# Half of O by wide matmuls, and sum p·dp by VectorE, in a one-query attention backward

One Trainium2 chip, one core of it. The metric is the device time of one execution, in microseconds (us); lower is better.

## The reference, cut to what matters

```python
B, H, Sq, Skv, Dh = 1, 32, 1, 8192, 128            # q, k, v, grad_out: bfloat16

def _fwd_reference(q, k, v):
    scores = jnp.einsum('bhqd,bhkd->bhqk', q, k) * q.shape[-1] ** -0.5
    attn = _softmax(scores, axis=-1)
    return jnp.einsum('bhqk,bhkd->bhqd', attn, v)

_out, _vjp = jax.vjp(_fwd_reference, q, k, v)
return (_out, *_vjp(grad_out))                     # O, dq, dK, dV
```

For every head one query meets 8192 keys. With p the softmax, O = p·V, dp = V·dO, ds = p·(dp − sum p·dp), dq = ds·K, and the outer products dK = ds⊗q and dV = p⊗dO. K and V are read (134 MB), dK and dV are written (134 MB). The sum of p·dp over the keys equals O·dO. The kernel before takes it as O·dO, the changed kernel as sum p·dp.

## The kernel before

A head is four 2 MB transfers: K and V in, dK and dV out. Each is cut into sixteen shares (the trace has sixteen completion records a transfer). I take each to be one DMA engine's: a share of 128 KB takes 4.87 us in the steady stretch, 27 GB/s, and sixteen of these are the 427 GB/s of the page. What waits for a transfer waits for its slowest share: in the changed kernel a store that waited for an earlier one was issued at 374.06 us, when that one's slowest share had landed at 374.0 and the next at 368.5. The parts that the argument touches:

```python
K_BUFS = 3
V_BUFS = 2
# ... (cut)
    for h in range(H + 1):
        p_ = h - 1
        if h < H:
            rows_bc(h)                     # q and dO broadcast to all partitions, copy qd on ScalarE
            for u in range(NCH):
                k_blocks(h, u)             # K transposes on VectorE, four of 1.2 us
            k_scores(h)                    # scores on TensorE
        # ... (cut)
        if h > 0:
            ds_of(p_)                      # needs O.dO of the head before, in m[:, 1]
            outer(p_, "dk", 0)             # dK in four parts on VectorE, then a 2 MB store
            dq_of(p_, 0)
        # ... (cut: softmax of head h, its maxima and sums across partitions)
        v_transposes(h, 0); v_transposes(h, 1); v_transposes(h, 2)       # fp32 transposes on TensorE
        contract(Vt[h], x["p"], x["m"][:, 2:3])      # O: 64 matmuls with one moving column each
        nc.scalar.copy(o_all[:, h:h + 1], x["m"][:, 2:3])
        v_scores(h, 0); v_scores(h, 1)               # dp
        v_transposes(h, 3)
        nc.tensor.matmul(x["m"][:, 1:2], lhsT=do_f[:, h:h + 1].to_broadcast([P, P]),
                         rhs=o_all[:, h:h + 1], start=True, stop=True)   # O.dO on every partition
        v_scores(h, 2); v_scores(h, 3)
        outer(h, "dv", 0); outer(h, "dv", 1); outer(h, "dv", 2)          # dV, then a 2 MB store
        load_v(h + 2)
        outer(h, "dv", 3)
```

Of the kernel before, what the change touches and what calls it, by code (L numbers as in the profile page):

```python
# [9 lines left out]
ALU = mybir.AluOpType  # L10
AX = mybir.AxisListType
BF16 = mybir.dt.bfloat16
F32 = mybir.dt.float32
PSUM = bass.MemoryType.PSUM

CH = 16
R = 4
K_BUFS = 3
V_BUFS = 2
QD = 32  # L20


@with_exitstack
def kernel(
# [11 lines left out]
    nc = tc.nc  # L36
    P = 128
    _, H, S, D = k.shape
    assert D == P and S % (P * CH) == 0 and H <= P
    NT = S // P  # L40
    NCH = NT // CH
# [4 lines left out]
    scale = float(D) ** -0.5  # L46

    consts = ctx.enter_context(tc.tile_pool(name="consts", bufs=1))
# [3 lines left out]
    tpool = ctx.enter_context(tc.tile_pool(name="tsb", bufs=3))  # L52
    gpool = ctx.enter_context(tc.tile_pool(name="gen", bufs=2))
    small = ctx.enter_context(tc.tile_pool(name="small", bufs=2))
    psT = ctx.enter_context(tc.tile_pool(name="psT", bufs=2, space=PSUM))
    psS = ctx.enter_context(tc.tile_pool(name="psS", bufs=1, space=PSUM))
    psD = ctx.enter_context(tc.tile_pool(name="psD", bufs=2, space=PSUM))
# [30 lines left out]
    ident = consts.tile([P, P], BF16)  # L88
# [31 lines left out]


    twice = consts.tile([H, 2, 2, W], BF16)
    do_f = consts.tile([P, H], F32)

    def do_columns():
        for e2 in range(2):
            nc.scalar.copy(
                twice[:, e2], rows[:, 1, :].rearrange("h (j e) -> h e j", e=2)[:, e2:e2 + 1, :].to_broadcast([H, 2, W]))
        tp = psT.tile([P, CH, P], BF16, tag="T", name="tp_do")
        for e2 in range(2):  # L130
            nc.tensor.transpose(tp[:, e2, 0:H], twice[:, e2].rearrange("h t j -> h (t j)"), ident[0:H, 0:H])
        nc.tensor.transpose(tp[:, 2, 0:H], rows[:, 1, :], ident[0:H, 0:H])
        for e2 in range(2):
            for t in range(2):
                nc.scalar.copy(do_blk[t * W:(t + 1) * W, :, e2, t], tp[t * W:(t + 1) * W, e2, 0:H])
        nc.scalar.copy(do_f[:], tp[:, 2, 0:H])

    o_all = consts.tile([P, H], F32)
    dq_all = consts.tile([P, H], F32)

    def k_blocks(h, u):


        if u == 0:
            XK[h] = ktpool.tile([P, CH, NB, NCH, QD], F32, tag="XK", name="XK_sb")
        nc.vector.transpose(XK[h][:, :, :, u, :],  # L146
                            slots(Kt[h], u, NCH).rearrange("p g d -> p (g d)").bitcast(F32).rearrange(
                                "p (g w j) -> p g w j", g=CH, w=NB))

    def k_scores(h):  # L150
        x = st[h]
        out = x["s"][:, 0:NT].rearrange("p (a g) -> p g a", a=NQ)
        cols = XK.pop(h).rearrange("p g w u i -> p (g w u i)").bitcast(BF16).rearrange(
            "p (g w ui e) -> p g w e ui", g=CH, w=NB, e=2)
        for g in range(CH):
            for c in range(2 * NB):
                nc.tensor.matmul(out[:, g, :], lhsT=cols[:, g, c // 2, c % 2], rhs=q_blk[:, h, c, :],  # L157
                                 start=(c == 0), stop=(c == 2 * NB - 1), skip_group_check=True)
# [18 lines left out]
    def v_transposes(h, c):  # L177

        T_ps = psT.tile([P, CH // 2, P], F32, tag="T", name="T_ps")
        words = Vt[h].rearrange("p n d -> p (n d)").bitcast(F32)  # L180
        for i in range(CH // 2):
            m = c * CH // 2 + i
            nc.tensor.transpose(T_ps[:, i, :], words[:, m * P:(m + 1) * P], ident_f[:])  # L183
        X = tpool.tile([P, CH // 2, P], F32, tag="XT", name="XT_sb")
        nc.scalar.copy(X[:], T_ps[:])  # L185
        XV[h, c] = X
# [11 lines left out]
    def contract(Xt, rep, out_col, first=0, last=NT):  # L198
        for n in range(first, last):
            nc.tensor.matmul(out_col, lhsT=Xt[:, n, :], rhs=rep[:, n, 0:1],  # L200
                             start=(n == 0), stop=(n == NT - 1), skip_group_check=True)

    def outer(h, which, r):
        x = st[h]
        if r == 0:
            x[which] = gpool.tile([P, NT, D], BF16, tag=which, name="G_" + which)
        G, dst = x[which], out_2 if which == "dk" else out_3
        rep, row = x["ds"] if which == "dk" else x["p"], x["qd"][:, 0 if which == "dk" else 1, :]
        Q = NT // 4
        nc.vector.tensor_tensor(  # L210
            slots(G, r, 4).rearrange("p n (a b) -> p n a b", b=R),
            slots(rep, r, 4).unsqueeze(2).to_broadcast([P, Q, D // R, R]),
            row.rearrange("p (a b) -> p a b", b=R).unsqueeze(1).to_broadcast([P, Q, D // R, R]),
            op=ALU.mult)
        parts = 1
        if h == 0 or h == H - 1:
            parts = 2
        if r % (4 // parts) == 4 // parts - 1:
            c = r // (4 // parts)
            nc.sync.dma_start(rows_of(dst, h, c, parts), slots(G, c, parts))  # L220
# [19 lines left out]
    def dq_of(h, half):  # L240
        out = st[h]["dp"][:, 128:129]
        contract(Kt[h], st[h]["ds"], out, half * NT // 2, (half + 1) * NT // 2)
        if half == 1:
            nc.scalar.copy(dq_all[:, h:h + 1], out)  # L244
# [10 lines left out]
    for h in range(H + 1):  # L255
        p_ = h - 1
        if h < H:
            x = st[h] = {}
            rows_bc(h)
            for u in range(NCH):  # L260
                k_blocks(h, u)
            k_scores(h)
        if h == 0:
            do_columns()
        if h > 0:
            ds_of(p_)
            outer(p_, "dk", 0)
            dq_of(p_, 0)
        if h < H:
            s_mask(h)  # L270
            s_swap(h)
        if h > 0:
            dq_of(p_, 1)
            outer(p_, "dk", 1)
        if 0 < h and h + 2 < H:
            load_k(h + 2)
        if h < H:
            mx = small.tile([P, 1], F32, tag="mx")
            nc.vector.reduce_max(mx[:], x["sn"], axis=AX.X)
            top = small.tile([P, 1], F32, tag="top")  # L280
            nc.vector.tensor_scalar_mul(top[:], mx[:], scale)
            x["m"] = psM.tile([P, 512], F32, tag="m", name="m_ps")
            nc.tensor.transpose(x["m"][:, 128:256], top[:].to_broadcast([P, P]), ident_f[:])
        if h > 0:
            outer(p_, "dk", 2)
        if h == 0:
            load_k(2)
        if h < H:
            nbias = small.tile([P, 1], F32, tag="nbias")
            nc.vector.tensor_reduce(nbias[:], x["m"][:, 128:256], axis=AX.X, op=ALU.max, negate=True)  # L290
            e = small.tile([P, NT], F32, tag="e")
            rs = small.tile([P, 1], F32, tag="rs")
            nc.scalar.activation(e[:], x["sn"], ACT.Exp, bias=nbias[:], scale=scale, accum_out=rs[:])  # L293
            nc.tensor.matmul(x["m"][:, 0:1], lhsT=ones_f[:], rhs=rs[:], start=True, stop=True,  # L294
                             skip_group_check=True)
        if h > 0:
            outer(p_, "dk", 3)
        if h == H:
            break
        rinv = small.tile([P, 1], F32, tag="rinv")  # L300
        nc.vector.reciprocal(rinv[:], x["m"][:, 0:1])  # L301
        x["p"] = small.tile([P, NT, R], BF16, tag="prep", name="p_rep")
        nc.scalar.activation(x["p"][:], e[:].unsqueeze(2).to_broadcast([P, NT, R]), ACT.Copy, scale=rinv[:])  # L303
        x["p_s"] = small.tile([P, NT], F32, tag="p_s", name="p_s")
        nc.vector.tensor_scalar(x["p_s"][:], e[:], rinv[:], scale, op0=ALU.mult, op1=ALU.mult)
        v_transposes(h, 0)
        v_transposes(h, 1)
        v_transposes(h, 2)
        contract(Vt[h], x["p"], x["m"][:, 2:3])
        nc.scalar.copy(o_all[:, h:h + 1], x["m"][:, 2:3])  # L310
        v_scores(h, 0)
        v_scores(h, 1)
        v_transposes(h, 3)
        nc.tensor.matmul(x["m"][:, 1:2], lhsT=do_f[:, h:h + 1].to_broadcast([P, P]), rhs=o_all[:, h:h + 1],
                         start=True, stop=True, skip_group_check=True)
        v_scores(h, 2)
        v_scores(h, 3)
        outer(h, "dv", 0)
        outer(h, "dv", 1)
        outer(h, "dv", 2)  # L320
        if 0 < h and h + 2 < H:
            load_v(h + 2)
        outer(h, "dv", 3)
        if h == 0:
            load_v(2)
        if h == H - 1:
            result(o_all, out_0)

    result(dq_all, out_1)
    order.__exit__(None, None, None)  # L330


# [28 lines left out]
```

## Time and profile before

| | before |
|---|---|
| time, median of the first three runs (range) | 646.29 us (646.24 to 646.5) |
| span of the profiled run, mean granted TensorE clock | 644.5 us, 0.600 |
| busy: TensorE, VectorE, ScalarE | 75%, 78%, 28% |
| data queue | 268.47 MB, 98.2% of sixteen engines |
| instruction queue (q8) | 75 packets, 1.23 MB |

A share of 98.2% over sixteen engines says that the transfers bound the kernel. It doesn't say which engine ends last, and that is what the time is. For that one reads the windows of the tail, where a share of 0.06 means one engine of sixteen.

One view that the prediction doesn't show becomes important. It is the chain of waits of the kernel before around 100 us (columns: start, duration, what ran):

```profile
101.31 0.58 PE m_ps L294 x2
101.90 4.09 PE T_ps L183 x24
105.98 1.59 PE m_ps L200 x64
...
117.49 0.35 PE dp_ps L200 x8
117.87 28.45 DMA Kt<-in_k_dram
146.34 4.62 DVE XK_sb L146 x4
```

Up to 117.9 us the chain goes through TensorE, ScalarE and VectorE: the first transfers run ahead, and compute sets the pace of the heads (17.2 us, from one exponential to the next). From there on, the chain goes through a wait for K in every second head, and a head takes 19.8 us. I call the two stretches "compute paces" and "transfers pace".

### The profile page before, as it was taken

The page shows a single profiled execution, that of the slowest core. Times are in us where ns is not written, and L with a number is a line of the kernel's source. Part 1 is how long each engine was busy: PE and PEld are TensorE (multiplying, and loading weights), DVE is VectorE, ACT ScalarE, POOL GpSimd, SP SyncE. Part 2 cuts the span into 40 slices and gives each one's busy share as a digit, 9 for nine tenths or more (in the row PEclk, how much of TensorE's full clock was granted, in tenths as well). Part 3 has the DMA queues.
Part 4 walks back from the last instruction along what each step waited for, and adds up shares of the span by engine and source line. Part 5 has one row for each costly group of instructions (what it writes and reads, how often), then busy time and mean ns, then how long its engine had stood idle before and what let it go on. Part 6 is the DMA issues. An engine that isn't in the chain of part 4 may idle for free.

```text
span 644.5 us, 20935 instructions
## 1 busy us (share of the span) xinstructions
PE 481.0 (75%) x9673; PEld 452.0 (70%) x9673; DVE 505.5 (78%) x653; ACT 183.5 (28%) x332; POOL 0.7 (0%) x6
## 2 busy tenths in 40 slices
PE   3898888886677877768777787667786777877780
PEld 2888888886677866768666777667785676866670
DVE  5989899867977779777788777797767977778860
ACT  2333333332233222233222332223322223222230
POOL 0000000000000000000000000000000000000000
PEclk9766666655666655666556666556655666655665
DMA  8999999999999999999999999999999999999985
GB/s 349 407 425 430 424 425 423 429 426 431 427 428 427 427 427 429 429 429 425 433 422 433 425 430 427 427 429 425 427 429 425 431 425 429 429 427 430 424 365 238
DMA packets 19718, 269.80 MB, mean 419 GB/s; under 512 B 2352, under 2 KB 2352, under 8 KB 2864
## 3 DMA queue, kind: packets, MB, share of 16 engines
q1 hardware_dynamic: 19584, 268.47, 98.2%
q8 instruction: 75, 1.23, 0.7%
q14 instruction: 11, 0.09, 0.0%
q10 hardware_dynamic: 48, 0.01, 0.0%
HBM read 134.23 MB, written 134.23 MB: 417 GB/s over the span
## 4 chain that ended last, share of the span: by engine, by line
DMA 59%; PE 21%; DVE 14%; ACT 2%; issue 1%; SPq 0%; DVEq 0%; ACTq 0%
DMA Kt<-in_k_dram 48%; DVE XK_sb L146 8%; PE T_ps L183 8%; DMA out_dram<-G_dv 5%; DMA out_dram<-G_dk 5%; PE s_ps L157 5%; DVE G_dk L210 4%; PE dp_ps L200 3%; PE m_ps L200 2%; PE dp_ps L195 2%; ACT XT_sb L185 1%; PE m_ps L294 1%; DVE G_dv L210 1%; PE s_ps L173 1%; DVE sm L163 1%
## 5 line engine op out<-in xcount | busy, mean ns | idle before, releaser
L210 DVE TENSOR_TENSOR G_dv<-p_rep,qd 128x2048 bf16<-128x2048 bf16 x128 | 148.2, 1221 | 90.3 <-DMA out_dram<-G_dv 84.6
L183 PE MATMUL T_ps<-ident_f,Vt 128*128 128x128 f32 x1024 | 203.4, 382 | 0.2 <-PE m_ps L294 0.2
L183 PEld LDWEIGHTS T_ps<-ident_f,Vt 128*128 128x128 f32 x1024 | 190.7, 210 | 0.2 <-issue 0.2
L185 ACT COPY XT_sb<-T_ps 128x1024 f32<-128x1024 f32 x128 | 128.6, 1013 | 129.3 <-PE T_ps L183 127.2
L210 DVE TENSOR_TENSOR G_dk<-ds_rep,qd 128x2048 bf16<-128x2048 bf16 x128 | 155.6, 1218 | 2.9 <-DMA out_dram<-G_dk 1.9
L146 DVE STREAM_TRANSPOSE XK_sb<-Kt 128x1024 f32<-128x1024 f32 x128 | 148.3, 1214 | 5.8 <-DMA Kt<-in_k_dram 4.7
L157 PEld LDWEIGHTS <-XK_sb 128*128 128x128 bf16 x2048 | 57.7, 104 | 90.7 <-DVE pdt L234 79.9
L157 PE MATMUL s_ps<-q_blk,XK_sb 128*128 128x4 bf16 x2048 | 59.7, 168 | 82.1 <-DVE pdt L234 72.1
L195 PE MATMUL dp_ps<-do_blk,XT_sb 128*128 128x2 bf16 x2048 | 66.7, 164 | 18.1 <-ACT XT_sb L185 18.1
L195 PEld LDWEIGHTS <-XT_sb 128*128 128x128 bf16 x2048 | 64.9, 102 | 20.7 <-ACT XT_sb L185 20.7
L200 PE MATMUL dp_ps<-ds_rep,Kt 128*128 128x1 bf16 x2048 | 64.1, 165 | 1.3 <-issue 1.0
L200 PEld LDWEIGHTS <-Kt 128*128 128x128 bf16 x2048 | 59.6, 104 | 6.8 <-issue 6.6
L244 ACT COPY dq_all<-dp_ps 128x1 f32<-128x1 f32 x32 | 5.1, 159 | 192.4 <-PE dp_ps L200 178.5
L200 PEld LDWEIGHTS <-Vt 128*128 128x128 bf16 x2048 | 57.7, 97 | 0.9
L200 PE MATMUL m_ps<-p_rep,Vt 128*128 128x1 bf16 x2048 | 56.9, 164 | 0.0
L294 PEld LDWEIGHTS m_ps<-rs,ones_f 128*128 128x128 f32 x64 | 16.0, 311 | 49.9 <-ACT e L293 49.9
L294 PE MATMUL m_ps<-rs,ones_f 128*128 128x1 f32 x64 | 18.8, 362 | 40.5 <-ACT e L293 40.5
L303 ACT ACTIVATE p_rep<-e,rinv 128x256 bf16<-128x256 f32 x32 | 16.3, 508 | 30.1 <-DVE rinv L301 30.1
L163 DVE TENSOR_TENSOR sm<-s_ps,in_quad 128x256 f32<-128x256 f32 x32 | 13.6, 424 | 11.1 <-PE s_ps L157 7.9
L229 ACT CAST qd<-s_ps 128x256 bf16<-128x256 f32 x32 | 11.9, 372 | 32.2 <-PE s_ps L225 32.2
L236 DVE SCALAR_TENSOR_TENSOR ds_rep<-dp_ps,pdt,p_s 128x256 bf16<-128x256 f32 x32 | 15.5, 484 | 5.2 <-PE dp_ps L195 2.4
L293 ACT ACTIVATE e<-s_ps,nbias 128x64 f32<-128x64 f32 x32 | 10.0, 313 | 31.8 <-DVE nbias L290 31.8
(44 smaller groups left out, 143.4 us busy)
## 6 DMA issues: line engine op xcount, KB each, us to landing
Vt<-in_v_dram SPq DMA_DIRECT2D x32, 2048.0 KB, 30.0
Kt<-in_k_dram SPq DMA_DIRECT2D x31, 2048.0 KB, 30.8
out_dram<-G_dv SPq DMA_DIRECT2D x30, 2048.0 KB, 34.6
out_dram<-G_dk SPq DMA_DIRECT2D x30, 2048.0 KB, 33.6
out_dram<-G_dv SPq DMA_DIRECT2D x4, 1024.0 KB, 15.0
out_dram<-G_dk SPq DMA_DIRECT2D x4, 1024.0 KB, 13.3
Kt<-in_k_dram SPq DMA_DIRECT2D x4, 512.0 KB, 5.1
out_dram<-fin_sb SPq DMA_DIRECT2D x2, 8.0 KB, 13.1
```

Source lines behind the costliest of these rows:

```text
L146: nc.vector.transpose(XK[h][:, :, :, u, :], slots(Kt[h], u, NCH).rearrange("p g d -> p (g d)").bitcast(F32).rearrange("p (g w j) -> p g w ...
L157: nc.tensor.matmul(out[:, g, :], lhsT=cols[:, g, c // 2, c % 2], rhs=q_blk[:, h, c, :], start=(c == 0), stop=(c == 2 * NB - 1), skip_group ...
L163: nc.vector.tensor_tensor(x["sm"][:], x["s"][:, 0:NT].rearrange("p (a g) -> p a g", a=NQ).unsqueeze(2) .to_broadcast([P, NQ, NCH, CH]), in ...
L183: nc.tensor.transpose(T_ps[:, i, :], words[:, m * P:(m + 1) * P], ident_f[:])
L185: nc.scalar.copy(X[:], T_ps[:])
L195: nc.tensor.matmul(st[h]["dp"][:, n:n + 2], lhsT=X[:, i, e2, :], rhs=do_blk[:, h, e2, :], start=(e2 == 0), stop=(e2 == 1), skip_group_chec ...
L200: nc.tensor.matmul(out_col, lhsT=Xt[:, n, :], rhs=rep[:, n, 0:1], start=(n == 0), stop=(n == NT - 1), skip_group_check=True)
L210: nc.vector.tensor_tensor(slots(G, r, 4).rearrange("p n (a b) -> p n a b", b=R), slots(rep, r, 4).unsqueeze(2).to_broadcast([P, Q, D // R, ...
L229: nc.scalar.copy(x["qd"][:].rearrange("p a d -> p (a d)"), x["s"][:, 256:512])
L236: nc.vector.scalar_tensor_tensor(out=x["ds"][:], in0=x["dp"][:, 0:NT].unsqueeze(2).to_broadcast([P, NT, R]), scalar=pdt[:], in1=x["p_s"][: ...
L294: nc.tensor.matmul(x["m"][:, 0:1], lhsT=ones_f[:], rhs=rs[:], start=True, stop=True, skip_group_check=True)
L303: nc.scalar.activation(x["p"][:], e[:].unsqueeze(2).to_broadcast([P, NT, R]), ACT.Copy, scale=rinv[:])
```

## The change

Its intent: fewer TensorE instructions (32 narrow O matmuls become 8 wide ones), and no dependence of ds on O. A wide matmul takes four keys' columns of p as weights and four tiles of V as 512 moving columns. Only the four diagonal 128-column blocks of the 4x512 result are O. They lie on four partitions, so they are sent through a DRAM scratch and summed once at the end. The last head keeps narrow matmuls and does them behind its dq.

```diff
+    def o_wide(h, first, last):
+        x = st[h]
+        for g in range(first, last):
+            nc.tensor.matmul(x["s"][0:R, :], lhsT=x["p"][:, R * g:R * (g + 1), 0],
+                             rhs=Vt[h][:, R * g:R * (g + 1), :].rearrange("p n d -> p (n d)"),
+                             start=(g == 0), stop=(g == WIDE // R - 1), skip_group_check=True)
+        if last == WIDE // R:
+            four = fours.tile([R, R * D], F32, tag="four", name="four")
+            nc.scalar.copy(four[:], x["s"][0:R, :])
+            nc.sync.dma_start(scratch[h, 0:R * R * D].rearrange("(a c) -> a c", a=R), four[:])
+    def pd_of(h):
+        # ... (cut: tiles)
+        nc.vector.tensor_tensor_reduce(out=junk[:], in0=x["p_s"][:], in1=x["dp"][:, 0:NT], scale=1.0,
+                                       scalar=0.0, op0=ALU.mult, op1=ALU.add, accum_out=pd[:])
+        nc.tensor.matmul(x["m"][:, 1:2], lhsT=ones_s[:], rhs=pd[:], start=True, stop=True, ...)
 # ... (cut; in the loop over the heads)
-            for u in range(NCH):
+            for u in range(NCH - 1):
                 k_blocks(h, u)
+        if h > 0:
+            pd_of(p_)
+        if h < H:
+            k_blocks(h, NCH - 1)
 # ...
         v_transposes(h, 1)
+        if h < H - 1:
+            o_wide(h, 0, 8)
         v_transposes(h, 2)
-        contract(Vt[h], x["p"], x["m"][:, 2:3])
-        nc.scalar.copy(o_all[:, h:h + 1], x["m"][:, 2:3])
+        if h < H - 1:
+            o_narrow(h, WIDE)
 # ...
-        nc.tensor.matmul(x["m"][:, 1:2], lhsT=do_f[:, h:h + 1].to_broadcast([P, P]), rhs=o_all[:, h:h + 1], ...)
 # ... (cut: behind V of the last head, the read-back; at the end, sum, transpose and store of O)
+            nc.sync.dma_start(blocks[0:h], scratch[0:h].rearrange("h (a c) -> h a c", a=R)[:, :, 0:D])
+    nc.vector.reduce_sum(block_sum[:], blocks[:].rearrange("h a d -> h d a"), axis=AX.X)
```

More of the change, by code (lines that the diff above doesn't have):

```diff
@@ L20 @@
 QD = 32
+WIDE = 32
 @with_exitstack
@@ L54 @@
     small = ctx.enter_context(tc.tile_pool(name="small", bufs=2))
+    fours = ctx.enter_context(tc.tile_pool(name="fours", bufs=3))
+    dram = ctx.enter_context(tc.tile_pool(name="scr", bufs=1, space=bass.MemoryType.DRAM))
     psT = ctx.enter_context(tc.tile_pool(name="psT", bufs=2, space=PSUM))
@@ L122 @@
     twice = consts.tile([H, 2, 2, W], BF16)
-    do_f = consts.tile([P, H], F32)
     def do_columns():
@@ L131, in do_columns @@
             nc.tensor.transpose(tp[:, e2, 0:H], twice[:, e2].rearrange("h t j -> h (t j)"), ident[0:H, 0:H])
-        nc.tensor.transpose(tp[:, 2, 0:H], rows[:, 1, :], ident[0:H, 0:H])
         for e2 in range(2):
@@ L135, in do_columns @@
                 nc.scalar.copy(do_blk[t * W:(t + 1) * W, :, e2, t], tp[t * W:(t + 1) * W, e2, 0:H])
-        nc.scalar.copy(do_f[:], tp[:, 2, 0:H])
+    ones_s = consts.tile([P, P], F32)
+    nc.vector.memset(ones_s[:], 1.0 / scale)
+    blocks = consts.tile([H, R, D], F32)
+    nc.vector.memset(blocks[:], 0.0)
+    scratch = dram.tile([H, R * (R + 1) * D], F32, name="scratch")
     o_all = consts.tile([P, H], F32)
@@ L201, in contract, with o_narrow @@
                              start=(n == 0), stop=(n == NT - 1), skip_group_check=True)
+    def o_wide(h, first, last):
[8 more added lines that the diff above has]
+            nc.sync.dma_start(scratch[h, 0:R * R * D].rearrange("(a c) -> a c", a=R), four[:])
+    def o_narrow(h, first):
+        x = st[h]
+        for n in range(first, NT):
+            nc.tensor.matmul(x["m"][:, 2:3], lhsT=Vt[h][:, n, :], rhs=x["p"][:, n, 0:1],
+                             start=(n == first), stop=(n == NT - 1), skip_group_check=True)
+        nc.scalar.copy(o_all[:, h:h + 1], x["m"][:, 2:3])
+    def pd_of(h):
+        x = st[h]
+        junk = small.tile([P, NT], F32, tag="junk")
+        pd = small.tile([P, 1], F32, tag="pd")
+        nc.vector.tensor_tensor_reduce(out=junk[:], in0=x["p_s"][:], in1=x["dp"][:, 0:NT], scale=1.0,
+                                       scalar=0.0, op0=ALU.mult, op1=ALU.add, accum_out=pd[:])
+        nc.tensor.matmul(x["m"][:, 1:2], lhsT=ones_s[:], rhs=pd[:], start=True, stop=True, skip_group_check=True)
     def outer(h, which, r):
@@ L273 @@
             dq_of(p_, 1)
+            if h == H:
+                o_narrow(p_, 0)
             outer(p_, "dk", 1)
@@ L313 @@
         v_transposes(h, 3)
-        nc.tensor.matmul(x["m"][:, 1:2], lhsT=do_f[:, h:h + 1].to_broadcast([P, P]), rhs=o_all[:, h:h + 1],
-                         start=True, stop=True, skip_group_check=True)
         v_scores(h, 2)
@@ L326 @@
         if h == H - 1:
-            result(o_all, out_0)
+            nc.sync.dma_start(blocks[0:h], scratch[0:h].rearrange("h (a c) -> h a c", a=R)[:, :, 0:D])
     result(dq_all, out_1)
+    block_sum = consts.tile([H, D], F32)
+    nc.vector.reduce_sum(block_sum[:], blocks[:].rearrange("h a d -> h d a"), axis=AX.X)
+    fin_ps = psT.tile([P, CH // 2, P], F32, tag="T", name="fin_o")
+    nc.tensor.transpose(fin_ps[0:H, 0, :], o_all[:], ident_f[:])
+    o_sb = consts.tile([H, D], BF16)
+    nc.vector.tensor_tensor(o_sb[:], fin_ps[0:H, 0, :], block_sum[:], op=ALU.add)
+    nc.sync.dma_start(out_0.rearrange("b h s d -> (b h s) d"), o_sb[:])
     order.__exit__(None, None, None)
```

## The prediction

The sum came to **647.4 us**, the mean of two cases. To the 646.3 us of before it added -0.9 for instruction packets, +2.9 for the scratch stores (31 times 84 + 9 ns, on four engines) and +3.2 for the read-back (124 times 26 ns, on one engine). The first case assumed without a trace that the read-back lies on one of the four engines of the stores and that this engine is one of the eight that carry instruction packets: 646.3 - 0.9 + 2.9 + 3.2, less 2.1, the average lead of a late engine on the latest, is 649.4. The second, "if not", gave 645.4. A sign that the first had come: a very low DMA share for several us at the end.

Three figures that the text takes for granted were measured in the traces of the two kernels. Wide matmuls of 512 columns start 427 ns apart at a granted clock of 0.5 and 216 ns at 1.0 (medians of 38 and 138 in the changed kernel), so eight are 3.4 and 1.7 us. There are 258 TensorE rows to an instruction packet before (19,384 to 75) and 256 after (17,894 to 70), and with five packets fewer went 1271 instructions fewer of all engines, 254 a packet. And the denser work was granted the full clock more often: 31 stretches of 6.8 us and one of 3.4, for 32 of 3.4 before, or 0.68 on average for 0.60.

> **What bounds the kernel now.** I read the page first (engine shares, slices, queues), then the windows of the tail, then the chain in order of time, then the packets of the trace. Lines of the page:
>
> ```profile
> PE 481.0 (75%) x9673; PEld 452.0 (70%) x9673; DVE 505.5 (78%) x653; ACT 183.5 (28%) x332; POOL 0.7 (0%) x6
> DMA  8999999999999999999999999999999999999985
> GB/s 349 407 425 430 424 425 423 429 426 431 427 428 427 427 427 429 429 429 425 433 422 433 425 430 427 427 429 425 427 429 425 431 425 429 429 427 430 424 365 238
> q1 hardware_dynamic: 19584, 268.47, 98.2%
> q8 instruction: 75, 1.23, 0.7%
> DMA 59%; PE 21%; DVE 14%; ACT 2%; issue 1%; SPq 0%; DVEq 0%; ACTq 0%
> L200 PE MATMUL m_ps<-p_rep,Vt 128*128 128x1 bf16 x2048 | 56.9, 164 | 0.0
> ```
>
> No compute engine is above 78%, and the DMA engines are busy from the second slice to the last but one, at about 427 GB/s. 268.47 MB at that rate are 629 us of a 644.5 us span, so only some 15 us are not plain transfer. The two last slices show where: 365 and 238 GB/s. The windows there (columns: PE, PEld, DVE, ACT, POOL busy, clock, DMA share, GB/s):
>
> ```profile
> 632.00:634.00 2.00, 0.00 (x0) 0.00 (x0) 0.00 (x0) 0.00 (x0) 0.00 (x0) 0.50 0.93 387
> 634.00:640.00 6.00, 0.00 (x0) 0.00 (x0) 0.00 (x0) 0.00 (x0) 0.00 (x0) 0.50 0.56 235
> 640.00:642.00 2.00, 0.00 (x0) 0.00 (x0) 0.00 (x0) 0.00 (x0) 0.00 (x0) 0.50 0.19 79
> ```
>
> From 634 to 640 us the share is 0.56 with nothing left to compute: about nine of sixteen engines still work and seven are done. The completion records of each transfer in the trace (sixteen, one an engine) say the same. At the first whole V they lie within 0.6 us of each other, at a transfer near 130 us within 4.7, near 330 within 9, and of the last dK store seven come at 633.7 and nine between 639.9 and 643. The lag grows in jumps of about 1.5 us, one about every 9 us, in turn on eight engines. That is the pace of the q8 packets (75 in 644 us, 16 KB each, 1.0 us a packet against 0.61 for a data packet; the data packet after one is also stretched to 1.0 to 1.1). So the end is set by **the slowest DMA engine**: its share of the data and its 8 to 10 instruction packets. Had it idle time? The tail of the chain says no:
>
> ```profile
> 608.95 0.02 DVEq L210
> 609.02 0.36 DVE G_dk L210
> 614.45 5.22 PE T_ps L183 x24
> 619.67 1.62 PE m_ps L200 x64
> 625.33 1.22 DVE G_dk L210
> 627.69 2.27 DVE G_dk L210 x2
> ```
>
> The last compute goes from a store's landing at 608.9 to the issue of dK of the last head at 627.7 (18.8 us). The slowest engine then still has six shares of 2 MB before that store, at 4.87 us each 29 us, to 638. Last-head compute has 10 us of slack.
>
> [...] The trace's clock is 0.60 on average (one 3.4 us window in five or six at full); 24 fp32 transposes took 5.13 us at half clock, 214 ns each[...].
>
> **The change part by part** (31 of 32 heads; the last keeps narrow matmuls).
> - *Removed on TensorE*: 32 of 64 narrow O matmuls a head. 56.9 / 2048 = 27.8 ns each, 0.89 us a head. Also the matmul of o with dO in its old place (L314, 0.23 to 0.43 us on the chain).
> - *Added on TensorE*: 8 matmuls of 512 columns: 3.4 us at half, 1.7 at full clock; I take 2.6 since they sit in the densest stretch. Net +1.7 us a head, PE busy about 530 us. Beside the transfers.
> - *VectorE*: a product-and-sum over 128x64, estimated 0.3 us from the 128x64 row of L305 (0.26) plus an accumulator read; 10 us in all, DVE about 515 us. It stands before the fourth K transpose and waits for dp. In a compute-bound head the fourth transpose (1.16) thus slips behind dp: about +0.85 us. In the steady state K arrives last, and it is +0.3.
> - *ScalarE*: a copy of 4x512 from PSUM, about 0.59 us between the rows of 256 (0.37) and 1024 columns (1.01). 18 us in all; idle anyway.
> - *Head period*: early heads, before the transfers pace them, ran every 17.2 us; steady ones every 19.8 (K loads of the chain at 155.1, 194.9, 234.5: 39.7 for two). With +1.7, +0.85, -0.3: 19.5. Just hidden, and the 10 us slack covers an excess of 0.3 us a head.
> - *Instruction packets*: TensorE's list shrinks from 16,660 to 15,200 rows; the other engines add about 190. (1460 - 190) / 256 = 5.0 packets fewer, 0.6 on each of eight engines, x 1.5 = **-0.9 us**. This is the change's whole gain on the bound.
> - *Scratch stores*: per head one 2 KB packet on four engines. 8 KB took 309 ns, 4 KB 159, so 2 KB about 84 plus 9 for the semaphore[...].
> - *Read-back*: [...] A 256 B packet took 18 ns, so about 26[...].
> - *Result O at the end*: sum, transpose and store follow the read-back, but its packet queues behind dK like the old result's: about 0. *O of the last head behind dq*: takes 1.6 us from a chain with slack: 0.
>
> [...] If not, the fast engines' 6 us of reserve (and what they starve anyway) swallow both: **645.4**. At half each: **647.4**.
>
> **The rivals.**
> (a) *Compute becomes the bound.* For it: a period of 19.5 beside 19.8 is close, and a head at half clock throughout would cost 0.8 more. Against it: denser work should be granted full clock more often, and the tail has 10 us of slack. At 20.3 us a head the compute would end 15 to 20 us later, minus the slack: 652 to 656. I give an effect over 2% 3 in 100.
> (b) *A wait in the DMA queue.* In the new order each transfer also waits for the eighth before it; with five a head instead of four, dV's store waits for dK's store of two heads before, which landed 5 us later than the old issue. For it: real waits will appear on SP. Against it: five 2 MB transfers (24 us) stay queued on the slowest engine, so it never starves. Worth 0 to 2 us.
> (c) *The designer's gain*: fewer instruction packets and an early last dK give 2 us or more (643 to 644). For it: the 1.5 us jumps are real. Against it: only five packets go, and the tail's chain has slack.
>
> **Range and chances.** The two cases give 645.4 and 649.4; the packet count per engine is worth a packet (1.5 us) either way; the small transfers may cost twice my estimate (+3), and (a) has a tail upward. Range 644.0 to 652.5. Beyond 2% would be 633 or 659: the first needs less data, the second (a) in full.
>
> **What would show each step.** Right: q8 falls from 75 to about 70 packets; GB/s stays near 427; the last windows still show half of the engines working alone; PE busy near 530. [...] Wrong: DMA share below 0.95 in mid-run, the chain full of PE and DVE rows instead of K loads, a head period of 20 or more, or q8 unchanged.

## The result, and the profile after

The changed kernel is correct and took **652.37 us** (median of 4, 651.64 to 652.71) beside 646.26 us for the kernel before in the same rounds. The ratio is 1.0095, 95% interval [1.0077, 1.0112]. A ratio is the mean time of one kernel's runs over that of the other's of the same rounds, so it is not quite the ratio of the medians. A change below 2% was foretold and came. The range held the time, but near its upper end: +6.1 us where +1.1 was predicted. That it held was luck: its upper part was kept for small transfers at twice their cost and for compute as the bound, and neither came.

The page of the changed kernel, the lines that answer to those shown of before:

```profile
PE 513.3 (79%) x8928; PEld 424.1 (65%) x8928; DVE 513.3 (79%) x721; ACT 198.8 (31%) x360; POOL 0.7 (0%) x6
GB/s 335 421 429 421 424 419 422 425 426 430 424 428 425 418 422 427 429 427 425 428 427 427 424 431 427 424 427 429 427 426 426 430 429 423 425 429 428 398 367 157
q1 hardware_dynamic: 19957, 268.79, 97.6%
q8 instruction: 70, 1.15, 0.7%
DMA 45%; PE 32%; DVE 13%; issue 4%; ACT 3%; SPq 0%; DVEq 0%; ACTq 0%
L212 PE MATMUL s_ps<-Vt,p_rep 128*4 128x512 bf16 x248 | 72.7, 446 | 0.0
L217 ACT COPY four<-s_ps 4x512 f32<-4x512 f32 x31 | 17.8, 576 | 39.1 <-PE s_ps L212 39.1
```

In mid-run the GB/s are what they were. They fall in the last slices: 398, 367, 157. On the chain, DMA has dropped from 59% to 45% and PE has risen from 21% to 32%. The windows of the tail (columns as in the prediction):

```profile
638.00:640.00 2.00, 0.00 (x0) 0.00 (x0) 0.23 (x1) 0.00 (x0) 0.00 (x0) 0.50 0.79 327
640.00:642.00 2.00, 0.00 (x0) 0.00 (x0) 0.00 (x0) 0.00 (x0) 0.00 (x0) 0.50 0.42 172
642.00:644.00 2.00, 0.00 (x0) 0.00 (x0) 0.00 (x0) 0.00 (x0) 0.00 (x0) 0.50 0.06 25
644.00:646.00 2.00, 0.00 (x0) 0.00 (x0) 0.00 (x0) 0.00 (x0) 0.00 (x0) 0.50 0.07 29
646.00:648.00 2.00, 0.00 (x0) 0.00 (x0) 0.00 (x0) 0.00 (x0) 0.00 (x0) 0.50 0.06 25
```

Before, nine engines shared the last stretch. Now **one engine works alone for over 6 us**, at 25 to 29 GB/s. The completion records agree. Of the last dK store's sixteen shares, before, the slowest came at 643.2 us, the next at 642.9 and the fastest at 633.9. After, the slowest came at 649.1, the next at 642.4 and the fastest at 639.2. Fifteen engines have ended by 642.4, a little sooner than before; the last one ends 5.9 us later than the last one did, and that is the change in time. I call this engine Y. The trace doesn't number the engines. But the landings of one transfer can be matched with those of the next (an inference, by the smallest changes): in the changed kernel three engines stay fast, four fall back from them by 4.0 to 8.5 us up to head 31, eight show seven to nine jumps of over 0.9 us, as an instruction packet leaves one (such a packet takes 1.0 us for the 611 ns of a data packet of the same 16 KB, and behind 66 of the 70, behind 74 of the 75 before, a data packet of over 0.9 us starts within 60 ns), and Y is the sixteenth. So I take the four to be those of the scratch stores, and Y not to be one of them; from 136 us on Y shows one such jump (at 395 us).

The landings show when Y falls behind. The times are completion records of the slowest share and the next, whichever engine's, of the same loads of V, in us:

| V of head | before: slowest | before: next | after: slowest | after: next |
|---|---|---|---|---|
| 4 | 75.3 | 74.6 | 74.8 | 74.7 |
| 7 | 136.0 | 135.1 | 136.3 | 135.1 |
| 10 | 196.1 | 194.9 | 197.6 | 195.1 |
| 13 | 255.5 | 254.7 | 259.3 | 255.0 |
| 19 | 374.3 | 374.2 | 378.9 | 374.9 |
| 25 | 493.9 | 493.8 | 499.1 | 493.3 |

From head 7 to head 13 the slowest share took (255.5 − 136.0) / 6 = 19.9 us a head before and (259.3 − 136.3) / 6 = 20.5 after. The next share kept its pace: 19.9 and 20.0. (Before head 7 several engines land within 0.3 us, and the slowest need not be Y.) From head 13 to head 25 the slowest took 19.9 and 20.0. So Y loses some 0.6 us a head up to about 260 us, which makes 3.8 of the 5.9 us by head 13; the rest comes more slowly behind it (4.6 by head 19, 5.2 by head 25).

The chain of waits after (columns: start, duration, what ran) shows what else ends there:

```profile
223.38 3.52 PE T_ps L188 x16
226.89 2.77 PE s_ps L212 x8
229.66 1.02 PE T_ps L188 x8
...
257.91 0.94 PE dp_ps L205 x32
258.88 30.43 DMA Kt<-in_k_dram
...
298.23 30.77 DMA Kt<-in_k_dram
```

Compute paces the heads until 258.9 us instead of 117.9. The wide matmuls (1.8 to 2.8 us for eight) stand on this chain. The period in that stretch is 18.3 and 19.3 us in turn, 18.8 on average, for 14 heads; before it was 17.2 us for seven.

### The profile page after: what moved, and what is told of

Its sections match the earlier page's. It is cut to its first block, busy times and chain, and to the rows that moved or that the text cites. A ratio compares the mean times of both kernels' runs of the same rounds, so it can differ in the third digit from the quotient of the medians. Undisturbed runs are those within 1.5% of the kernel's fastest.

```text
span 650.9 us, 19664 instructions
## 1 busy us (share of the span) xinstructions
PE 513.3 (79%) x8928; PEld 424.1 (65%) x8928; DVE 513.3 (79%) x721; ACT 198.8 (31%) x360; POOL 0.7 (0%) x6
## 4 chain that ended last, share of the span: by engine, by line
DMA 45%; PE 32%; DVE 13%; issue 4%; ACT 3%; SPq 0%; DVEq 0%; ACTq 0%
DMA Kt<-in_k_dram 44%; PE T_ps L188 12%; PE s_ps L162 7%; DVE XK_sb L151 6%; PE s_ps L212 5%; DVE G_dk L242 4%; PE dp_ps L200 3%; PE dp_ps L205 3%; ACT XT_sb L190 2%; PE m_ps L223 2%; PE m_ps L332 1%; DMA blocks<-scratch 1%; ACT e L331 1%; DVE sm L168 1%; PE s_ps L178 1%
## 5 line engine op out<-in xcount | busy, mean ns | idle before, releaser
L188 PE MATMUL T_ps<-ident_f,Vt 128*128 128x128 f32 x1024 | 185.0, 350 | 0.2 <-PE m_ps L332 0.2
L188 PEld LDWEIGHTS T_ps<-ident_f,Vt 128*128 128x128 f32 x1024 | 166.0, 190 | 13.9 <-issue 13.9
L162 PE MATMUL s_ps<-q_blk,XK_sb 128*128 128x4 bf16 x2048 | 59.8, 168 | 27.0 <-DVE pdt L266 18.7
L200 PEld LDWEIGHTS <-XT_sb 128*128 128x128 bf16 x2048 | 60.9, 97 | 28.2 <-ACT XT_sb L190 27.7
L212 PE MATMUL s_ps<-Vt,p_rep 128*4 128x512 bf16 x248 | 72.7, 446 | 0.0
L332 PE MATMUL m_ps<-rs,ones_f 128*128 128x1 f32 x64 | 18.7, 359 | 40.6 <-ACT e L331 40.3
L212 PEld LDWEIGHTS <-p_rep 128*4 128x4 bf16 x248 | 21.1, 95 | 44.8 <-issue 30.4
L233 PE MATMUL m_ps<-pd,ones_s 128*128 128x1 f32 x64 | 17.2, 338 | 23.0 <-DVE pd L231 22.1
L233 PEld LDWEIGHTS m_ps<-pd,ones_s 128*128 128x128 f32 x64 | 14.5, 282 | 30.5 <-DVE pd L231 30.5
L223 PEld LDWEIGHTS <-Vt 128*128 128x128 bf16 x1056 | 31.3, 96 | 0.3
L223 PE MATMUL m_ps<-p_rep,Vt 128*128 128x1 bf16 x1056 | 31.2, 163 | 0.0
L217 ACT COPY four<-s_ps 4x512 f32<-4x512 f32 x31 | 17.8, 576 | 39.1 <-PE s_ps L212 39.1
```

The costliest lines, as they stand in the source:

```text
L162: nc.tensor.matmul(out[:, g, :], lhsT=cols[:, g, c // 2, c % 2], rhs=q_blk[:, h, c, :], start=(c == 0), stop=(c == 2 * NB - 1), skip_group ...
L188: nc.tensor.transpose(T_ps[:, i, :], words[:, m * P:(m + 1) * P], ident_f[:])
L200: nc.tensor.matmul(st[h]["dp"][:, n:n + 2], lhsT=X[:, i, e2, :], rhs=do_blk[:, h, e2, :], start=(e2 == 0), stop=(e2 == 1), skip_group_chec ...
L212: nc.tensor.matmul(x["s"][0:R, :], lhsT=x["p"][:, R * g:R * (g + 1), 0], rhs=Vt[h][:, R * g:R * (g + 1), :].rearrange("p n d -> p (n d)"), ...
L217: nc.scalar.copy(four[:], x["s"][0:R, :])
L223: nc.tensor.matmul(x["m"][:, 2:3], lhsT=Vt[h][:, n, :], rhs=x["p"][:, n, 0:1], start=(n == first), stop=(n == NT - 1), skip_group_check=True)
```

## The experiments

Four theories:

- **S**: the extra transfers (scratch, read-back) or their waits in the DMA queue cost the time.
- **L**: the denser TensorE work (higher clock, more reading of V) slows the transfers.
- **P**: a longer compute chain, by whatever means, lets compute pace more heads, and Y falls back while it does.
- **D**, a cause for P: in that stretch few transfers are queued, and Y suffers from the shallow queue.

The expectations of the first four runs call L and P together C.

Each run was timed in three rounds against the kernel before (646.13, 646.22, 646.34 and 646.07 us in the four calls). All results were correct except that of e8.

### e1_fold: the change without its DRAM scratch

```diff
-            nc.sync.dma_start(scratch[h, 0:R * R * D].rearrange("(a c) -> a c", a=R), four[:])
+    # in o_narrow: fold the diagonal blocks into the same PSUM column
+            for a in range(R):
+                nc.tensor.matmul(x["m"][:, 2:3], lhsT=x["four"][:, a * D:(a + 1) * D], rhs=ident[0:R, a:a + 1], ...)
```

> The changed kernel with the scratch in DRAM taken out: the four diagonal blocks are added up on the chip by four small bf16 matmuls a head into the column of the narrow O; four transfers a head again, everything else of the change kept. Theory S (the extra transfers make one of the sixteen DMA engines late, 649.1 us for its last dK share in the changed kernel against 642.4 for the next): 645.0 to 646.0 us, the late engine within 1 us of the others. Theory C (the denser compute per head, which paces the heads until 255 us instead of 118, makes it late): 650 to 652 us with the same lone engine at the end.

Measured: 652.88 us (652.36 to 653.6), ratio 1.0102 [1.0087, 1.0117]. Compute paces until 259 us; the slowest share lands at 649.1 us, the next at 641.8. S falls: no scratch, no read-back, and the same time (C had named 650 to 652, so it is 0.9 us above).

The waits of SyncE's queue say the same of rival (b). They are first those of the changed kernel (two longer ones for compute are cut), then those of e1 (columns: what was waited for, us in total, times, longest); the waits for a dK or dV store that had not landed are gone in e1, and the time is not better.

```profile
...
SPq L252 <- DMA out_dram<-G_dk: 75.3, 19, 4.7
...
SPq L218 <- DMA out_dram<-G_dv: 59.7, 18, 3.9
```

```profile
SPq L80 <- PE T_ps L184: 264.5, 30, 9.8
SPq L76 <- PE m_ps L320: 200.3, 29, 9.5
SPq L251 <- DVE rinv L338: 77.3, 31, 11.1
SPq L251 <- DVE G_dv L241: 29.8, 4, 13.9
```

### e2_pd_only: only the sum p·dp on VectorE, and the last head's order

```diff
+        if h > 0:
+            pd_of(p_)          # between the third and the fourth K transpose, O stays narrow
```

> The kernel before with only the sum p*dp on VectorE and O of the last head behind its dq: no wide matmuls, no scratch. S: 646 us, as before. C, if the later fourth K transpose were what matters: 647 to 649; if the wide matmuls: 646. Instruction packets stay at 75.

Measured: 648.95 us (648.37 to 649.15), ratio 1.0039 [1.0024, 1.0054]. Period 18.0 us for eight heads, compute paces until 139 us; slowest 645.6, next 642.9. This part alone costs some 2.7 us, again at Y.

### e3_scratch_only: the kernel before with 31 scratch stores

```diff
+        if h < H - 1:
+            nc.sync.dma_start(scratch[h, 0:R * R * D].rearrange("(a c) -> a c", a=R), four_c[:])   # a constant tile
```

> The kernel before plus one scratch store of 4x512 a head from a constant tile, not read back (results stay right): the added transfers alone. S: 650 to 652 us with one engine alone at the end. C: 646 to 647 us; the four engines of the scratch get 3 to 4 us later but were 6 us ahead.

Measured: 646.03 us (645.62 to 646.57), ratio 0.9996 [0.9981, 1.0011]; slowest 643.1, next 642.8. The scratch stores cost nothing. The tail is that of before, with nine engines at work up to 640 us:

```profile
636.00:638.00 2.00, 0.00 (x0) 0.00 (x0) 0.00 (x0) 0.00 (x0) 0.00 (x0) 0.50 0.57 239
638.00:640.00 2.00, 0.00 (x0) 0.00 (x0) 0.00 (x0) 0.00 (x0) 0.00 (x0) 0.50 0.52 218
640.00:642.00 2.00, 0.00 (x0) 0.00 (x0) 0.00 (x0) 0.00 (x0) 0.00 (x0) 0.50 0.20 83
```

### e4_pe_load: the kernel before with the eight wide matmuls added and unused

```diff
+            for g in range(8):
+                nc.tensor.matmul(x["s"][0:R, :], lhsT=x["p"][:, R * g:R * (g + 1), 0],
+                                 rhs=Vt[h][:, R * g:R * (g + 1), :].rearrange("p n d -> p (n d)"), ...)
```

> The kernel before plus the eight wide matmuls a head into the spare bank, their result unused, no scratch, no instruction saved (two packets more): the TensorE load alone, 2 to 3 us a head. S: 646 to 648 us. C: 650 us or more, and the heads are paced by compute beyond 200 us.

Measured: 653.17 us (652.57 to 653.79), ratio 1.0106 [1.0089, 1.0123]. Period 18.3 to 19.5 us for 15 heads, compute paces until 278 us; slowest 650.1, next 642.4. Clock 0.68. The wide matmuls alone bring the whole loss. (The two packets more of the expectation are an estimate: 496 TensorE rows more, at the 258 a packet of the kernel before.) This fits L and P alike, since they load TensorE and lengthen the chain; e5 separates the two.

### e5_act_delay: a pure delay, no work added on TensorE

```diff
-        nc.scalar.copy(x["qd"][:].rearrange("p a d -> p (a d)"), x["s"][:, 256:512])
+        for _ in range(7):
+            nc.scalar.copy(x["qd"][:].rearrange("p a d -> p (a d)"), x["s"][:, 256:512])
```

> The kernel before with its 0.37 us copy of the q and dO rows on ScalarE repeated six times more at each head: 2.2 us of pure delay in each head's chain ahead of the K scores while compute paces, no work for TensorE, VectorE or the transfers, hidden behind K's landing when transfers pace. If the longer compute pace as such is the cause (theory P): compute paces until 200 us or later, one engine alone at the end, 649 to 653 us. If the load on TensorE is (theory L): 646 to 647 us, compute paces longer but the late engine is not later.

Measured: 653.39 us (653.19 to 654.49), ratio 1.0113 [1.0098, 1.0128]. Clock 0.603 as before, period 19.5 to 19.8 us in most heads to the end, no wait for K on the chain after the first load; slowest 651.4, next 643.3. The page and the tail:

```profile
PE 477.0 (73%) x9673; PEld 450.8 (69%) x9673; DVE 503.7 (77%) x653; ACT 255.3 (39%) x524; POOL 0.7 (0%) x6
PE 58%; ACT 20%; DVE 16%; issue 2%; DMA 1%; DVEq 0%; SPq 0%; ACTq 0%
```

```profile
640.00:642.00 2.00, 0.00 (x0) 0.00 (x0) 0.00 (x0) 0.00 (x0) 0.00 (x0) 0.50 0.98 410
642.00:644.00 2.00, 0.00 (x0) 0.00 (x0) 0.00 (x0) 0.00 (x0) 0.00 (x0) 0.50 0.26 98
644.00:646.00 2.00, 0.00 (x0) 0.00 (x0) 0.00 (x0) 0.00 (x0) 0.00 (x0) 0.50 0.06 25
646.00:648.00 2.00, 0.00 (x0) 0.00 (x0) 0.00 (x0) 0.00 (x0) 0.00 (x0) 0.50 0.07 29
648.00:650.00 2.00, 0.00 (x0) 0.00 (x0) 0.00 (x0) 0.00 (x0) 0.00 (x0) 0.50 0.06 25
```

L falls as the sole cause: six more ScalarE copies a head, with TensorE doing exactly what it did at the clock it had, give a lone engine again and a larger loss (0.4 us above the range that P had named). P stands, with two limits. The delay is not free of work: ScalarE's busy time rises from 183.5 to 255.3 us. And the landings show no steady loss: the slowest share of V took 20.2 us a head from head 7 to 13, 20.1 from 13 to 19, 20.0 from 19 to 25 and 20.6 from 25 to 31, though compute paces them all. Of the 7.0 us by which it is later than in the kernel before at head 31, 3.8 came in the last six heads.

### e6_pd_late: e2 with the sum behind the fourth K transpose

```diff
+            k_blocks(h, NCH - 1)
         if h > 0:
             pd_of(p_)
-        if h < H:
-            k_blocks(h, NCH - 1)
```

> The sum of p*dp on VectorE and the last head's order alone, as in e2 (648.95), but with the sum after the fourth K transpose instead of before it, so that transpose no longer waits for dp. P: the compute pace ends at about 118 us or sooner again and the time falls to 645.5 to 646.5. L: as e2 within 0.5, 648.5 to 649.5, if e2's loss came from the VectorE operation itself.

Measured: 647.63 us (647.38 to 647.72), ratio 1.002 [1.0005, 1.0035]. Period 17.2 to 17.8 us for seven heads; slowest 644.3, next 643.3. Half of e2's loss came from holding the fourth K transpose until dp was there. Both theories missed: P had named 645.5 to 646.5 and an end of the compute pace at 118 us or sooner (it is 136), L 648.5 to 649.5. The operations are e2's, only their order differs, and the loss halves: that speaks for the chain.

### e7_fold_pd_late: the same move in e1

The edit is e6's, in e1's kernel.

> e1 (wide matmuls, fold on the chip, 652.9) with the sum after the fourth K transpose. P: the pace ends before e1's 259 us, near 180, and the time falls to 648 to 651. L: stays within 0.7 of 652.9, as the TensorE load is the same.

Measured: 652.35 us (652.25 to 652.47), ratio 1.0093 [1.0076, 1.011]. Compute paces until 219 us instead of 259; slowest 649.2, next 641.7. The stretch was shorter and the loss was not, or by 0.5 us at most. P had named 648 to 651 and missed; what came is what L had named, within 0.7 us of e1. So the loss is not proportional to the length of the stretch, and of P only this much is left: a longer chain is enough for a loss (e5).

### e8_no_o: e6 without any O matmul (wrong: O is zero)

```diff
         if h < H - 1:
-            o_narrow(h, 0)
+            pass
```

> e6 without any O matmul: the first output is wrong on purpose (zeros). Takes 1.6 us out of each head's chain and some 16 of the 75 instruction packets. P: the pace by compute ends before 118 us, the lone engine finishes 1 to 2 us before 643.2 and the eight with the instruction packets 3 us before 642.9: 643.5 to 645. L says the same of the packets; if the late engine stays at 643 the time stays at 645.5 to 646.3.

Measured: 644.5 us (644.05 to 645.1), ratio 0.9973 [0.9958, 0.9987]. Period 16.9 us for six heads, compute paces until 99 us, q8 59 packets; slowest 640.9, next 640.5. A shorter chain and fewer instruction packets bring the end forward. With sixteen packets fewer, two for each of eight engines at 1.5 us, 3 us would be the most from that side, and the next-slowest engine is 2.4 us earlier than before.

### e9_fold_v3, e10_before_v3, e11_delay_v3: a third V buffer

The same edit in e1, in the kernel before and in e5:

```diff
-V_BUFS = 2
+V_BUFS = 3
```

> e1 (wide matmuls, fold on the chip, 652.9 us) with three V buffers instead of two, so that a V load no longer waits for TensorE to leave the buffer and is issued some 8 us earlier. Nothing computed changes. If the late engine is late because few transfers are queued while compute paces (theory D: from issue to last landing it is 13 to 20 us then, 31 when transfers pace): 647 to 650 us, the lone engine less late. If the pace as such matters (P without D): 652 to 653.

Measured: 652.57 us (651.76 to 652.71), ratio 1.0093 [1.0078, 1.0108]; slowest 649.5, next 642.0.

> The kernel before with three V buffers. D: its seven compute-paced heads have a deeper queue, the lone engine 1 to 2 us earlier, but the eight engines with the instruction packets end at 642.9 as before: 645.5 to 646.3. P without D: 646.2.

Measured: 646.19 us (646.01 to 646.35), ratio 0.9997 [0.9982, 1.0012]; slowest 643.2, next 642.7.

> e5 (pure delay on ScalarE, 653.4 us, compute paces all heads at 19.6 us) with three V buffers. D: 647 to 650 us. P without D: 653 to 654.

Measured: 654.14 us (653.7 to 654.57), ratio 1.0119 [1.0103, 1.0136]; slowest 651.1, next 642.9.

D gets no support. The buffer did deepen the queue, but only a little: from a transfer's issue to its first landed share it was 11.8 us on average for the transfers issued at 40 to 80 us in e1 and 15.2 in e9, 13.5 and 16.3 at 80 to 120, and 16.6 and 17.6 at 160 to 200; 11.2 and 14.0 at 40 to 80 in e5 and e11. The loss stayed as it was. In the kernel before it is 22.5 us at 80 to 120, so a queue as deep as that was not tried.

### e12_store_act: the changed kernel with stores issued by ScalarE

```diff
-            nc.sync.dma_start(rows_of(dst, h, c, parts), slots(G, c, parts))
+            nc.scalar.dma_start(rows_of(dst, h, c, parts), slots(G, c, parts))
```

> The changed kernel with the whole-head stores of dK and dV issued by ScalarE into a queue of their own instead of SyncE's, so that loads and stores no longer stand in one list and no load's issue stands behind a store's wait. The order of the instructions that compute stays. Theory P (the late engine falls back for as long as compute paces the heads, whatever the issue looks like): K waits appear on the chain only after some 240 to 270 us again, one engine ends 5 to 8 us after the next, time 651 to 653 as the changed kernel (652.4). Theory Q (it falls back because a store released by compute stands in the same list ahead of the loads, so that its packets meet the others' loads): the late engine is within 2 us of the next, time 644 to 647. A time above 655 would say that the two queues share the engines worse than one does.

Measured: 656.04 us (654.99 to 656.38), ratio 1.015 [1.0133, 1.0167]. A wait for K is on the chain from 183 us, the later heads take 20.3 us for 19.9 in the changed kernel, and the last head's exponential comes at 626.8 us instead of 618.7. A line of the end of its chain of waits, and two of the windows of its tail:

```profile
637.79 4.63 DVE G_dk L242 x4
...
648.00:650.00 2.00, 0.00 (x0) 0.00 (x0) 0.00 (x0) 0.00 (x0) 0.00 (x0) 0.50 0.06 26
650.00:652.00 2.00, 0.00 (x0) 0.00 (x0) 0.00 (x0) 0.00 (x0) 0.00 (x0) 0.50 0.07 29
```

The last dK is only made at 642.4, and the stores then take until 652. The time is above the 655 for which I had named "two queues share the engines worse than one does"; whether the second queue itself does that was not separated. From 648 to 652 one engine works alone again. Q (Y falls back because stores stand in one list ahead of the loads) had named at most 2 us between it and the next, so the run doesn't support Q. Because K itself came late, it is no clean test of P. No version here beats the kernel before with a correct O.

### All runs side by side

"Head period" is the mean of the first six, from one exponential to the next. "First wait" is the first long wait for a transfer on the chain; "slowest" and "next" are the landings of the last dK store's shares. e12 is left out, since with two queues I could not assign its records to transfers.

| run | time, us | head period, us | first wait, us | slowest | next | slowest − next |
|---|---|---|---|---|---|---|
| e8 | 644.5 | 17.0 | 99 | 640.9 | 640.5 | 0.4 |
| before | 646.26 | 17.3 | 118 | 643.2 | 642.9 | 0.3 |
| e10 | 646.19 | 17.5 | 126 | 643.2 | 642.7 | 0.5 |
| e3 | 646.03 | 17.4 | 135 | 643.1 | 642.8 | 0.3 |
| e6 | 647.63 | 17.5 | 136 | 644.3 | 643.3 | 1.0 |
| e2 | 648.95 | 17.9 | 139 | 645.6 | 642.9 | 2.7 |
| e7 | 652.35 | 18.7 | 219 | 649.2 | 641.7 | 7.5 |
| after | 652.37 | 18.9 | 259 | 649.1 | 642.4 | 6.7 |
| e1 | 652.88 | 18.8 | 259 | 649.1 | 641.8 | 7.3 |
| e9 | 652.57 | 19.0 | 268 | 649.5 | 642.0 | 7.5 |
| e4 | 653.17 | 18.9 | 278 | 650.1 | 642.4 | 7.7 |
| e5 | 653.39 | 19.6 | none | 651.4 | 643.3 | 8.1 |
| e11 | 654.14 | 19.5 | 580 | 651.1 | 642.9 | 8.2 |

Broadly, the longer compute paces, the later the slowest engine; the next engine stays within 641.7 and 643.3, but for e8. The first wait is a poor measure, though: e3, e6 and e2 have it at 135, 136 and 139 us and end 0.1 us earlier, 1.1 and 2.4 us later than the kernel before. The early head period orders the runs better: 17.5 us or less goes with 640.9 to 644.3 for the slowest share, 17.9 with 645.6, 18.7 to 19.0 with 649.1 to 650.1, and 19.5 and 19.6 with 651.1 and 651.4. A longer period also makes the stretch longer, so these runs don't separate the two.

## Why the prediction was right, and where it failed

- *The bound.* "The slowest DMA engine": held, but it was the wrong engine. The prediction counted nine late engines in the tail and eight that carry instruction packets, and did not ask about the ninth. Matched from landing to landing in the kernel before, eight engines show eight to ten jumps of over 0.9 us and end by 642.9. The one that ends last, at 643.2, shows four, none after 211 us, and falls back in small steps, as Y does. So such an engine was there before, only 0.3 us after the next, and the packets saved on the others, the "whole gain on the bound", could not bring the end forward while it ended last. (The landings of the last dK store read 633.9 and 640.1 to 643.2, some 0.2 us later than the prediction gives them.)
- *TensorE and VectorE.* PE busy was put at about 530 us and came to 513.3. The eight wide matmuls took 72.7 / 31 = 2.35 us a head, close to the 2.6. That is 293 ns a matmul at a mean clock of 0.68, between the 427 at 0.5 and the 216 at 1.0. The difference is mostly that other work took less time with the clock at 0.68 for 0.60: the fp32 transposes fell from 203.4 to 185.0 us (in both kernels they start 213 ns apart at 0.5 and 109 at 1.0, medians). VectorE's 515 was 513.3; the ScalarE copy, put at 0.59 us, took 0.576.
- *Instruction packets.* 75 to 70 as worked out. (The trace has 19,384 TensorE rows before and 17,894 after, not 16,660 and 15,200; the difference, 1490, is near the 1460.) The next-slowest share comes 0.5 us earlier than before, the sign right and the size near the 0.9.
- *Scratch and read-back.* The 31 stores of four rows were 124 packets of 2 KB, with four completion records each, and the read-back was 124 packets of 512 B with one record; I take these for four engines and one. A 2 KB packet took 84 ns as estimated, and the four engines that carry the stores moved by 3.5 to 4.9 us against the fastest, for the 2.9. The read-back packets took 27 ns each (median) and all started within 3.1 us. Both were near in size and fell on engines that had reserve; e3 and e1 show that they cost no time. So of the two cases of the prediction the cheaper one held, the one that said 645.4. It was wrong by 7.0 us, and the average of the two cases hid this.
- *The step that failed* is the overlap: "Just hidden, and the 10 us slack covers an excess of 0.3 us a head." The head period was even below the estimate (18.8 us for the 19.5), and the slack was there. But I had asked only whether a longer chain is shorter than the transfers' pace. It also moves the time at which the transfers begin to pace, here from 118 to 259 us, and in that stretch one engine takes 20.5 us for a head's shares instead of 19.9. The missing term, as measured in the changed kernel, is that 0.6 us a head: 3.5 us in the six heads from 7 to 13, and some 2 us that came in smaller steps behind it. That a longer chain brings such a loss is shown by e5 with a delay and no change on TensorE, by e4 with the wide matmuls alone, by e2 with the sum alone. That the loss is 0.6 us for every head that compute paces is not shown: e5's came unevenly, and e7's shorter stretch saved 0.5 us at most.
- *Rivals.* (a), compute becoming the bound, named a time of 652 to 656 and is nearest, but by a period of 20.3 us that did not come (18.8), and the last head's compute was not what ended late. (b)'s waits are real, 75.3 and 59.7 us on SyncE's queue, and cost nothing (e1). The first are those that the prediction named: dV's stores at 354.1, 374.1 and 394.9 us were issued just when dK's store eight places earlier in the queue had landed (354.0, 374.0 and 394.8). The second are the scratch stores', for a dV. (c) is out: 652, not 644.
- *Signs.* "The chain full of PE and DVE rows instead of K loads" was listed as a sign of being wrong, and it came, up to 259 us. The very low share for several us came too, but not on the engines for which I had listed it. "The last windows still show half of the engines working alone" was to show the bound, and did not come.

Not settled: why this one engine loses time when compute paces. The scratch (e3) and TensorE's load (e5) are not needed for it, and the jumps of instruction packets are almost absent from its landings. A queue some 3 us deeper didn't help. Where Y's packets can be followed from one to the next in the changed kernel (most shares of 2 MB from 259 us on), those of loads take 611 to 625 ns and those of stores 611 to 742, where 611 is the median of all; in the last six heads of e5 those of stores reach 766. That tells where the time goes and not why.

## What to carry to other kernels

In this kernel, bound by transfers, work that hides below the transfers' pace still cost time (+6.1 us; a mere delay, e5, +7.2): it slowed the heads that compute paces (18.8 us for 17.2) and prolonged that phase (to 259 us from 118). So ask how long and how fast that phase is as well as whether it exists. Ask which DMA engine ends last and read the completions share by share; sums over sixteen engines hid it until the tail (425 to 429 GB/s in every 100 us from 100 to 600, in the kernel before, the changed one and e1 to e4). A delay of the same length without the work (e5) separates "more TensorE work" from "later" in one run.
